# Turning q and k of batch 3 and the dilated half of batch 2 on the crossbar instead of the array

## The chip, the cores and the metric

One core of one Trainium2 chip. The metric is the device time of one launch in microseconds (us), median of several executions. PE is TensorE, DVE is VectorE, ACT is ScalarE, POOL is GpSimd, SP is SyncE. PSUM is the memory that TensorE's results go to here, SBUF the one that all other tiles of the program lie in.

## The reference

```python
# q, k, v: (8 batches, 8 heads, 576 tokens, 64)
scores = q @ k.T / 8
# heads 0-3: causal window of 32 keys; heads 4-7: 32 keys, every 4th ("dilated", window 128)
attn = softmax(where(mask, scores, -1e9))
x = (attn @ v)                   # -> (4608 tokens, 512)
h = maximum(x @ w_in, 0)         # 512 -> 2048
out = (h * h) @ w_out            # 2048 -> 512
```

All matmuls are in bf16 with f32 sums. The FFN (the last two lines) is by far the larger part; attention is woven between its pieces.

## The kernel before

Eight heads are four pairs (`e`): pairs 0 and 1 near, 2 and 3 dilated. A program in text says what is done between two FFN pieces; `|` parts the pieces. `2q1` turns and copies the queries of batch 2 (the third), pair 1; `k` does keys, `v` spreads values, `a` and `b` are the scores of the first and the second half, `o` and `p` the weighted sums of the two halves. `L3:q...` loads q and k of batch 3, and `L3:x` turns them on the crossbar (a DMA that transposes). The order within each engine's queue is the order of this program; nothing reorders it.

q and k arrive with tokens on partitions and must be turned. The kernel before does that on TensorE's array for batches 0 to 3 and by crossbar from batch 4 on (`XB = 4`):

```python
rb = [{nm: const.tile([80, ...], bf16, name=f"{nm}b{i}") for nm in "qk"} for i in range(2)]   # staging
ps_f = tile_pool(name="ps_f", bufs=4, PSUM)   # FFN sums
ps_a = tile_pool(name="ps_a", bufs=2, PSUM)   # array transposes, scores
ps_o = tile_pool(name="ps_o", bufs=1, PSUM)   # weighted sum "po"
ps_d = tile_pool(name="ps_d", bufs=1, PSUM)   # its denominators "pd"
...
def trans(b, e, nm, part):               # array: 8 transposes into one PSUM tile, then 4 copies
    ps = ps_a.tile([P, 1024], bf16, name="pa")
    copy = nc.scalar.copy if nm == "q" and e < NE // 2 else nc.vector.tensor_copy
    ...
def pv(b, e, part):                      # weighted sum and softmax denominator
    o, d = ps_o.tile(...), ps_d.tile(...)
    for ...: nc.tensor.matmul(o, v, p)           # "po"
    for ...: nc.tensor.matmul(d, ones, p)        # "pd"
    nc.scalar.activation(rec, d, Ln)
    nc.scalar.activation(rec, rec, Exp, scale=-1.0)
    nc.vector.tensor_tensor(out=xT, in0=o, in1=rec, op=mult)   # frees o
...
def step(b, code):
    if what in "qk" and b >= XB:         # crossbar: only the 4 copies, out of SBUF
        halves(e, what, (qx if what == "q" else kx)[...], 0, M, nc.vector.tensor_copy)
    elif what in "qQkK": trans(...)
```

The softmax here doesn't subtract the row's maximum and nothing guards it: scores larger than these inputs give would overflow.

Of the kernel before, what the change touches and what calls it, by code (L numbers as in the profile page):

```python
# [12 lines left out]
RES = 4  # L13
# [5 lines left out]


PROGRAM = (
    "L0:q023 L0:q00 L0:q01 0k0 L0:q10123 0q0 0q1 0k1 L0:v0pd 0a0 0q2 L0:i0 0a1 0k3 L0:v1dpr 0k2 0q3 0Q1 "
    "0K3 0a3 0Q3 0K2 0a2 0v2 0Q0 L0:i1 L0:o2 0K0 0o0 0v3 0b0 0Q2 0o2 0K1 0b3 0o1 L0:o0 0o3 0V3 0b2 0b1 | "
    "0V2 | 0p0 | 0p1 0p2 | L0:o1 0p3 L0:o3 | | | y | | | | | | | | L1:q00123 z | | | | | L1:v0dp "
    "L1:q10123 | | L2:qw0123 L1:v1dpr 1q1 1q3 | 1q2 | 1k2 | 1k1 1v3 | 1a2 | 1v2 1k0 1q0 | 1o2 | 1a0 1a1 | "
    "1k3 1o0 1o1 | 1a3 1Q0 | 1K0 1o3 | 1Q1 1K1 | 1Q2 | 1b0 | | 1Q3 1K2 L2:vwpdr | | | 2q0 | | 2k0 1V2 | "
    "1b2 1p0 | 1b1 1V3 1K3 | | 1p2 1p1 | 2a0 1b3 | 2k1 2o0 2b0 1p3 | 2q1 2k2 | | L3:qw0123 2q2 2p0 "
    "L3:vwpdr 2a1 | | | 2b1 | 2v2 2o1 2q3 2a2 | | 2p1 | 2k3 | 2b2 2o2 | 2v3 | 2a3 2p2 L4:q10123 | 2b3 | "
    "3k1 2o3 3q1 | | 3a1 L4:q00123 2p3 | 3k0 3k2 | | 3o1 | | | 3q0 3v2 | | | | 3a0 | 3b1 3k3 | | | 3p1 "
    "L4:x 3q2 | | 3b0 | 3a2 3q3 3o0 4k0 | | | 3o2 3b2 | | 3p0 3v3 | 4q1 3a3 | 3p2 4q2 4q0 | L5:q10123 3b3 "  # L30
    "| 3o3 L4:vwpdr | 4k1 | | L5:q00123 3p3 4k2 4k3 4a0 L5:vwpdr | | | 4b0 | | 4q3 | | 4o0 | | | 4a2 4v2 "
    "| 4b2 | 4a3 L5:x 4a1 | 4o2 | | | 4p2 L6:q00123 4v3 | | 4b1 | | 4p0 | | 4p1 | 5q0 5k0 | 4b3 | | | | "
    "4o1 | | 5k2 L6:q10123 4o3 | 5q2 5k1 | | 4p3 | 5q1 |"
)


# [24 lines left out]
def kernel(  # L61
# [9 lines left out]
    nc = tc.nc  # L71
    P = nc.NUM_PARTITIONS
    B, H, S, D = q.shape
# [3 lines left out]
    bf16 = mybir.dt.bfloat16  # L77
# [5 lines left out]
    NE = H // 2  # L83
# [3 lines left out]
    M = S // RES  # L87
    MS = (0, 64)
    MN = (64, M - 64)
    NT = 512  # L90
    NTILES = NTOK // NT
    XB = 4
    WHOLE = tuple(range(2, XB))
    PARTED = (0, 1)
    ADDED = 4
    RING = 4 * S
    KT = DM // P
# [2 lines left out]
    const = ctx.enter_context(tc.tile_pool(name="const", bufs=1))  # L100
# [26 lines left out]
    ]  # L127
    w_out_sb = const.tile([P, NF, DM], bf16, name="w_out_sb")
    xT = const.tile([P, KT, RING], bf16, name="xT")
    rb = [{nm: const.tile([80, 2 * H * RES * D], bf16, name=f"{nm}b{i}") for nm in "qk"} for i in range(2)]  # L130
    qT = const.tile([P, NE, RES, M], bf16, name="qT")

    qx = const.tile([P, H, 2, M], bf16, name="qx")
    kx = const.tile([P, H, 2, M], bf16, name="kx")
    kbd = const.tile([P, NE, NB, P], bf16, name="kbd")
    vbd = [const.tile([P, NE, NB, P], bf16, name=f"vbd{i}") for i in range(2)]

# [5 lines left out]
    def staged(b: int, nm: str):  # L143


        t = rb[b % 2][nm]
        if b in WHOLE:
            return t[:, :].rearrange("p (h a x) -> p h a x", h=H, a=2)
        return t[:, :].rearrange("p (a h x) -> p a h x", h=H, a=2)

    def load_qk(b: int, part, es):
        hs = slice(2 * es[0], 2 * es[-1] + 2)
        for nm, src in (("q", q), ("k", k)):
            t = staged(b, nm)
            if b in WHOLE:
                nc.gpsimd.dma_start(
                    t[0 : M // 2, hs, :, :].rearrange("p h a x -> p (h a) x"),
                    src[b, hs, :, :].rearrange("h (a p r) d -> p (h a) (r d)", a=2, r=RES),
                )
            else:  # L160
                t0, n = RES * MS[part], MN[part]
                nc.gpsimd.dma_start(  # L162
                    t[0:n, part, hs, :], src[b, hs, t0 : t0 + RES * n, :].rearrange("h (p r) d -> p h (r d)", r=RES)
                )

    def load_v(b: int, parts, which="pdr"):

# [45 lines left out]

    def cross(b: int, nm: str, part: int):

        n, m0 = MN[part], MS[part]
        nc.sync.dma_start_transpose(
            (qx if nm == "q" else kx)[:, :, :, m0 : m0 + n].rearrange("p h c m -> p (h c) m"),
            staged(b, nm)[0:n, part, :, :].rearrange("p h x -> p (h x)"),
        )  # L220

    def trans(b: int, e: int, nm: str, part: int):

        ps = ps_a.tile([P, 1024], bf16, name="pa")
        t = staged(b, nm)
        copy = nc.scalar.copy if nm == "q" and e < NE // 2 else nc.vector.tensor_copy
        if b == 0:

            m0, n = MS[part], MN[part]
            pv_ = ps[:, 0 : RES * n].rearrange("p (r m) -> p r m", r=RES)  # L230
            for r in range(RES):
                for hl in range(2):
                    nc.tensor.transpose(  # L233
                        pv_[64 * hl : 64 * hl + 64, r, :],
                        t[0:n, part, 2 * e + hl, D * r : D * r + D],
                        ident[0:n, 0:n],
                    )
            if nm == "q":
                copy(qT[:, e, :, m0 : m0 + n], pv_)
                return  # L240
            for hl in range(2):
                rows = slice(64 * hl, 64 * hl + 64)
                if e < NE // 2:
                    copy(  # L244
                        kbd[rows, e, m0 // 16 : (m0 + n) // 16, rows].rearrange("p i (m r) -> p i m r", r=RES),
                        pv_[rows, :, :].rearrange("p r (i m) -> p i m r", m=16),
                    )
                else:
                    copy(kbd[rows, e, RES * part : RES * part + RES, rows], pv_[rows, :, 0:64])  # L249
                    if part:  # L250
                        copy(
                            kbd[rows, e, 8, rows].rearrange("p (m r) -> p m r", r=RES),
                            pv_[rows, :, 64:n].rearrange("p r m -> p m r"),
                        )
            return
        if b in WHOLE:
            m0, n, pitch, cuts = 0, M, M, [(t[0:72, :, a, :], 72 * a, 72) for a in range(2)]
        else:

            m0, n, pitch, cuts = MS[part], MN[part], 80, [(t[0:80, part, :, :], 0, 80)]  # L260
        pv_ = ps[:, 0 : 4 * pitch].rearrange("p (h c m) -> p h c m", h=2, c=2)
        for hl in range(2):
            for c in range(2):
                for src, c0, w in cuts:
                    nc.tensor.transpose(  # L265
                        pv_[:, hl, c, c0 : c0 + w], src[:, 2 * e + hl, P * c : P * c + P], ident[0:w, 0:w]
                    )
        halves(e, nm, pv_[:, :, :, 0:n], m0, n, copy)
# [31 lines left out]
    def blocks(b: int, e: int, part: int):  # L300
# [3 lines left out]
        if e < NE // 2:  # L304
# [4 lines left out]
            return [(3, None, 64, 72)] + [(i, None, 16 * i, min(16 * i + 24, M)) for i in range(4, NB)]  # L309
        if b not in PARTED:  # L310
            rs = (2 * part, 2 * part + 1)
# [60 lines left out]
    def pv(b: int, e: int, part: int, spare=None, name=""):  # L372
# [8 lines left out]
        c = half_at(b, e)[0] * part  # L381
        byr = dil and b not in PARTED
        mms, dms = [], []
# [78 lines left out]
    def step(b: int, code: str):  # L462



        what, e = code[0], int(code[1])
        part = int(what in "QKVbp")
        if what in "qk" and b >= XB:
            t = qx if what == "q" else kx
            halves(e, what, t[:, 2 * e : 2 * e + 2, :, :], 0, M, nc.vector.tensor_copy)  # L470
        elif what in "qQkK":
            trans(b, e, what.lower(), part)
        elif what in "vV":
            spread_v(b, e, [part] if b in PARTED else [0, 1])
        elif what in "ab":
            scores(b, e, part, *((ps_f, "pf") if b == 0 and not part else ()))
        elif b == 0 and part and e % 2:
            pv(b, e, part, ps_a, "pa")
        elif b in PARTED and e % 2:
            pv(b, e, part, ps_f, "pf")  # L480
        else:
            pv(b, e, part)
# [140 lines left out]
    def run(code):  # L623
        if code == "y":
            for nm in "qk":
                nc.vector.memset(staged(1, nm)[64:80, 0, :, :], 0.0)
        elif code == "z":
            zero_halves(vbd[1])
        elif code[0] != "L":
            step(int(code[0]), code[1:])  # L630
        else:
            b, what, part, which = int(code[1]), code[3], code[4:5], code[5:]
            if what == "q":
                load_qk(b, None if part == "w" else int(part), [int(e) for e in which])
            elif what == "x":
                cross_all(b)
            elif what == "v":
                load_v(b, [0, 1] if part == "w" else [int(part)], which)
            else:
                (load_w_in if what == "i" else load_w_out)(int(part))  # L640
# [66 lines left out]
```

## Time and profile before

| | before |
|---|---|
| time, median of 3 runs | 319.62 us (319.12 to 319.97) |
| span of the profiled execution | 317.3 us |
| array transposes of batches 2 and 3 | 128 |

The page's slices of VectorE and ScalarE:

```profile
DVE  6785758898987987996599658965896324204400
ACT  5366735877958966686468646864686466316511
```

One slice is 7.9 us. From the 8th to the 12th slice (55 to 95 us) VectorE stands at 8 or 9 tenths and ScalarE at 5 to 9, while TensorE, shown in the prediction, stands at 9. The transposes that the change removes stand between 78.6 and 115.7 us, half of them in this stretch.

### The profile page before, as it was taken

To read this page: it belongs to the slowest core of one execution; us is meant where nothing else is said; L and a number is where in the kernel's file an instruction comes from. 1 tells how busy PE (TensorE), PEld (TensorE's weight loads), DVE (VectorE), ACT (ScalarE), POOL (GpSimd) and SP (SyncE) were. 2 spreads that over 40 slices of the span, in tenths; PEclk is the share of its full clock that TensorE was granted. 3 is DMA by queue.
4 is the path that set the end of the run, shared out by engine and by line. 5 is a ranking of instruction groups with operands and counts; after the bars stand their busy time and mean duration, and the time that the engine had idled before them with its cause. 6 is when DMAs were issued, how large, how long until landed. Compare 5 with 4: busy or idle time off the path is not lost.

```text
span 317.3 us, 6743 instructions
## 1 busy us (share of the span) xinstructions
PE 299.7 (94%) x2523; PEld 190.3 (60%) x2556; DVE 208.6 (66%) x664; ACT 195.4 (62%) x422; POOL 84.1 (27%) x130
## 2 busy tenths in 40 slices
PE   1698999999999999999999999999999999999995
PEld 1587945877965555555579755555555555445543
DVE  6785758898987987996599658965896324204400
ACT  5366735877958966686468646864686466316511
POOL 8762282367320037741271041000000000000000
PEclk9999999999999999999999999999999999999999
DMA  7999999999996619999699864352200210021022
GB/s 96 179 123 212 207 144 204 130 91 162 108 119 130 120 16 204 159 186 167 91 132 174 134 99 90 49 103 68 66 2 2 68 66 0 24 78 33 0 68 66
DMA packets 73056, 33.08 MB, mean 104 GB/s; under 512 B 44096, under 2 KB 67008, under 8 KB 73024
## 3 DMA queue, kind: packets, MB, share of 16 engines
q0 software_dynamic: 48096, 18.36, 50.3%
q1 hardware_dynamic: 24784, 14.16, 19.0%
q8 instruction: 20, 0.33, 0.4%
q10 hardware_dynamic: 144, 0.13, 0.1%
q14 instruction: 12, 0.10, 0.1%
HBM read 36.83 MB, written 9.44 MB: 146 GB/s over the span
## 4 chain that ended last, share of the span: by engine, by line
PE 88%; DVE 5%; ACT 3%; issue 2%; DMA 1%; POOL 1%; ACTq 0%; DVEq 0%; POOLq 0%
PE pf L529 38%; PE pf L561 37%; PE po L443 3%; PE pd L445 3%; PE pa L265 2%; PE pa L334 2%; PE pa L340 1%; DMA kb<-in_k_dram 1%; DVE xT L458 1%; PE pa L233 1%; DVE kbd L244 1%; DVE kbd L249 1%; ACT rec L447 1%; ACT qT L278 1%; ACT rec L448 1%
## 5 line engine op out<-in xcount | busy, mean ns | idle before, releaser
L529 PE MATMUL pf<-xT,w_in 128*128 128x256 bf16 (+1 forms) x758 | 132.9, 325 | 1.2 <-DVE xT L458 0.3
L561 PE MATMUL pf<-w_out_sb,h2T 128*128 128x512 bf16 (+1 forms) x569 | 131.0, 373 | 1.7 <-ACT osb L567 0.5
L529 PEld LDWEIGHTS <-w_in 128*128 128x128 bf16 x768 | 82.1, 114 | 35.7 <-issue 1.3
L540 ACT ACTIVATE h2T<-pf 128x512 bf16<-128x512 f32 x144 | 83.4, 597 | 24.7 <-PE pf L529 23.8
L561 PEld LDWEIGHTS <-h2T 128*128 128x128 bf16 x592 | 54.2, 98 | 53.5 <-issue 0.7
L541 DVE TENSOR_TENSOR h2T<-h2T 128x512 bf16<-128x512 bf16 x144 | 57.3, 422 | 36.0 <-ACT h2T L540 34.8
L567 ACT COPY osb<-pf 128x512 f32<-128x512 f32 (+1 forms) x37 | 21.2, 573 | 44.5 <-PE pf L561 41.5
L458 DVE TENSOR_TENSOR xT<-po,rec 128x288 bf16<-128x288 f32 (+2 forms) x56 | 25.5, 456 | 34.8 <-ACT rec L448 34.2
L447 ACT ACTIVATE rec<-pd 128x288 f32<-128x288 f32 (+2 forms) x56 | 23.1, 412 | 28.1 <-PE pd L445 28.0
L179 POOL DMA_DIRECT2D vbd<-in_v_dram x40 | 28.2, 728 | 43.8 <-PE pd L445 34.6
L344 ACT ACTIVATE pt<-pa 128x352 bf16<-128x352 f32 (+6 forms) x60 | 29.7, 502 | 8.4 <-PE pa L340 4.4
L448 ACT ACTIVATE rec<-rec 128x256 f32<-128x256 f32 (+2 forms) x64 | 28.4, 444 | 2.0
L443 PEld LDWEIGHTS <-vbd 128*128 128x128 bf16 x332 | 19.6, 99 | 10.2 <-issue 1.4
L443 PE MATMUL po<-pt,vbd 128*128 128x32 bf16 (+3 forms) x286 | 19.6, 199 | 0.7 <-DVE xT L458 0.7
L445 PE MATMUL pd<-pt,mk 128*128 128x96 bf16 (+5 forms) x172 | 18.0, 207 | 0.0
L162 POOL DMA_DIRECT2D qb<-in_q_dram x14 | 10.1, 721 | 27.0 <-PE po L443 24.6
L192 POOL DMA_DIRECT2D vd<-in_v_dram x24 | 14.7, 648 | 9.6 <-DMA kb<-in_k_dram 9.6
L278 DVE COPY qT<-qx 64x288 bf16<-64x288 bf16 x64 | 16.1, 251 | 0.8
L282 DVE COPY kbd<-kx 64x288 bf16<-64x288 bf16 x32 | 15.0, 469 | 0.4
L198 POOL DMA_DIRECT2D vbd<-in_v_dram x16 | 9.7, 617 | 17.4 <-PE pd L445 5.1
L334 PE MATMUL pa<-qT,kbd 128*128 128x96 bf16 (+2 forms) x160 | 13.8, 206 | 0.5 <-DVE kbd L244 0.4
L445 PEld LDWEIGHTS <-mk 128*128 128x128 bf16 x232 | 13.7, 99 | 0.7 <-issue 0.5
(60 smaller groups left out, 231.0 us busy)
## 6 DMA issues: line engine op xcount, KB each, us to landing
out_dram<-osb SPq DMA_DIRECT2D x18, 128.0 KB, 4.8
vd<-in_v_dram POOLq DMA_DIRECT2D x32, 64.0 KB, 5.2
w_in<-in_moe_w_in_dram POOLq DMA_DIRECT2D x2, 1024.0 KB, 9.0
w_out_sb<-in_moe_w_out_dram POOLq DMA_DIRECT2D x4, 512.0 KB, 13.5
qb<-in_q_dram POOLq DMA_DIRECT2D x6, 320.0 KB, 5.1
kb<-in_k_dram POOLq DMA_DIRECT2D x6, 320.0 KB, 6.6
vbd<-in_v_dram POOLq DMA_DIRECT2D x24, 72.0 KB, 5.8
out_dram<-osb SPq DMA_DIRECT2D x10, 160.0 KB, 2.2
```

The lines of the kernel that those rows point to most:

```text
L179: nc.gpsimd.dma_start(dst[rows, e, i0:i1, rows], v[b, 2 * e + hl, 64 * i0 : 64 * i1, :].rearrange("(i p) d -> p i d", p=64),)
L344: nc.scalar.activation(pt[:, off : off + n], ps[:, 0:n], ACT.Exp, scale=SCALE)
L443: nc.tensor.matmul(oo, vb[:, e, i, :], rh, start=(x == 0), stop=(x == len(mms) - 1), skip_group_check=True)
L445: nc.tensor.matmul(dd, ones[:, :], rh, start=(x == 0), stop=(x == len(dms) - 1), skip_group_check=True)
L447: nc.scalar.activation(rec[:, 0:n], d[:, 0:n], ACT.Ln)
L448: nc.scalar.activation(rec[:, 0:n], rec[:, 0:n], ACT.Exp, scale=-1.0)
L458: nc.vector.tensor_tensor(out=tok, in0=o if o is o3 else o[:, 0:n], in1=rec if o is o3 else rec[:, 0:n], op=ALU.mult)
L529: nc.tensor.matmul(acc[u][:, nt * x + y0 : nt * x + y1], w_in_sb[piece][:, kt, c0 : c0 + 509 : 4], xT[:, kt, t0 : t0 + y1 - y0], start=(kt ...
L540: nc.scalar.activation(hv, acc[u][:, :].rearrange("p (x n) -> p x n", x=per), ACT.Relu)
L541: nc.vector.tensor_tensor(out=hv, in0=hv, in1=hv, op=ALU.mult)
L561: nc.tensor.matmul(cur[m][:, c0:c1], h2[:, f, P * m : P * m + P], w_out_sb[:, f, c0:c1], start=(f == 0), stop=(f == NF - 1),)
L567: nc.scalar.copy(osb[:, c0:c1], cur[m][:, c0:c1])
```

## The change

Its intent: batch 3 wholly and the dilated half of batch 2 are turned by crossbar, so 96 array transposes leave TensorE. A third pair of staging buffers lets their loads come early enough; batch 2's remaining array transposes take 80 rows like batch 1's, so that there is only one layout of staging.

```diff
-    XB = 4
-    WHOLE = tuple(range(2, XB))
+    XB = 2
+    STAGE = (0, 1, 0, 2, 2, 2, 0, 1)
-    rb = [... for i in range(2)]
+    rb = [... for i in range(3)]
-    qx = const.tile(...); kx = const.tile(...)
+    qx = [const.tile(..., name=f"qx{i}") for i in range(2)]; kx = [...]      # by b % 2
 def cross(b, nm, part):
+    h0 = H // 2 if b == XB else 0                       # batch 2: dilated heads only
 def trans(...):
-        if b in WHOLE: cuts = [(t[0:72, :, a, :], 72 * a, 72) for a in range(2)]
+        if b == 2:     cuts = [(t[0:80, a, :, :], MS[a], 80) for a in range(2)]
 def step(...):
-        if what in "qk" and b >= XB:
+        if what in "qk" and (b > XB or b == XB and e >= NE // 2):
+            by_act = what == "q" and e < NE // 2 and b < ADDED         # near q of batch 3: ScalarE
 ...
+                nc.vector.memset(staged(2, nm)[64:80, 0, 0 : H // 2, :], 0.0)
 PROGRAM (loads and crossbars only; the order of attention steps is unchanged):
-  L2:qw0123 ... L2:vwpdr | | | 2q0 ... 2q1 2k2 | | L3:qw0123 2q2 2p0 L3:vwpdr ... 3q2 ... 3o3 L4:vwpdr
+  L2:q00123 L2:q10123 ... L2:vwpdr L3:q00123 L3:q10123 | L2:x | | 2q0 ... 2q1 2k2 L3:x | | 2q2 2p0 L3:vwpdr ... 3q2 L4:vwpdr ... 3o3
```

## The prediction

> **What bounds the kernel now.** I read the page first (busy shares and the slices), then the chain that ended last, then the groups by shape, then the waits, and last the order of time of the queues that start transfers.
>
> ```profile
> PE 299.7 (94%) x2523; PEld 190.3 (60%) x2556; DVE 208.6 (66%) x664; ACT 195.4 (62%) x422; POOL 84.1 (27%) x130
> PE   1698999999999999999999999999999999999995
> PEclk9999999999999999999999999999999999999999
> DMA  7999999999996619999699864352200210021022
> ...
> PE 88%; DVE 5%; ACT 3%; issue 2%; DMA 1%; POOL 1%; ACTq 0%; DVEq 0%; POOLq 0%
> ```
>
> PE is at nine tenths or more in every slice from about 32 us to the last one, at the full clock, and the chain is PE for 88%. A busy PE can hide waits, because the end of a matmul is modelled, so I checked it in the chain in order of time. In each line there: start, length, instructions.
>
> ```profile
> 50.76 0.29 PE pa L265 x8
> ...
> 99.82 0.52 PE pa L265 x16
> ...
> 211.54 2.59 PE pf L561 x12
> ```
>
> Twelve FFN matmuls of 512 columns take 2.59 us, 216 ns each, back to back. The array transposes (L265) are no different: 16 of the 72-row ones take 0.52 us, 32.5 ns each, and 8 of the 80-row ones (second batch) 0.29 us, 36 ns each. So behind the start-up (PE's one wait for a load is 6.4 us at the very start, below) nothing but PE work counts. What leaves PE's stream shortens the kernel by its back-to-back time; what leaves another engine gives nothing by itself.
>
> ```profile
> PE pa L233 <- DMA kb<-in_k_dram: 6.4, 1, 6.4
> ...
> L265 PE MATMUL pa<-mk,qb 72*128 72x72 bf16 x64 | 3.4, 196 | 0.0
> L265 PE MATMUL pa<-mk,kb 72*128 72x72 bf16 x64 | 3.2, 197 | 0.0
> ```
>
> The rows by shape say 196 ns for one such transpose. That is its latency. The last column, idle time of PE before it, is 0.0.
>
> **What the Trainium skill says.** "TensorE: Matmul & The Clock Gate", section "Back-to-back issue gap", gives N / 2.4 + 2.5 ns for a warm stream: 32.5 ns at 72 columns, 35.8 at 80, 215.8 at 512. The trace agrees (32.5, 36, 216). The same page, "Part 4: PE-mode transpose", gives 275 to 390 ns for one 128x128 transpose and says that the full clock does not engage for it; the trace does not show that cost in a stream: 197 ns of latency, 32.5 ns of pitch. "DMA: Bandwidth & Descriptors", section "Issuing engines are not separate DMA queues", says that transfers issued from any engine run on the same 16 DMA engines and interleave. So crossbar transposes compete with the loads. The trace agrees: with little beside it a crossbar occupies SP's queue 1.3 to 2.0 us, in the midst of loads up to 6.2 us.
>
> ```profile
> 100.13 1.34 SPq L217 DMA_TRANSPOSE kx<-kb  x1
> 101.65 1.76 SPq L217 DMA_TRANSPOSE qx<-qb  x1
> 103.52 1.99 SPq L217 DMA_TRANSPOSE kx<-kb  x1
> 105.61 1.97 SPq L217 DMA_TRANSPOSE qx<-qb  x1
> ...
> 138.66 6.21 SPq L217 DMA_TRANSPOSE kx<-kb  x1
> ```
>
> "VectorE: DVE Perf Modes", section "Why PSUM operands drop a tier", says that a PSUM source leaves VectorE one read port, so the copy loses its fastest mode. The rows agree in part: the contiguous copies gain some 50 ns from an SBUF source, the strided one for near keys hardly.
>
> ```profile
> L278 DVE COPY qT<-qx 64x288 bf16<-64x288 bf16 x64 | 16.1, 251 | 0.8
> L278 DVE COPY qT<-pa 64x288 bf16<-64x288 bf16 x16 | 4.9, 304 | 0.2
> L289 DVE COPY kbd<-kx 64x256 bf16<-64x256 bf16 x32 | 7.4, 230 | 0.3
> L289 DVE COPY kbd<-pa 64x256 bf16<-64x256 bf16 x16 | 4.6, 287 | 0.4
> L282 DVE COPY kbd<-kx 64x288 bf16<-64x288 bf16 x32 | 15.0, 469 | 0.4
> L282 DVE COPY kbd<-pa 64x288 bf16<-64x288 bf16 x16 | 7.7, 480 | 0.8 <-PE pa L265 0.3
> ```
>
> **The change, part by part.** I count batches from 0, so the third is batch 2.
>
> 1. Removed from PE. In the kernel before, batches 2 and 3 are turned on the array: per pair of heads and per q or k, 2 heads x 2 column halves x 2 row halves = 8 transposes, so 64 a batch (the 128 of the two 72-row rows). Batch 3 loses all 64, batch 2 its dilated half, 32. The program confirms it: 192 rows fewer on PE, 96 transposes and 96 weight loads. 96 x 32.5 ns = 3.12 us, all on the path. The order of the rest of PE's stream is the same.
> 2. Made longer on PE. The 32 transposes left for batch 2 go from 72 to 80 rows: 32 x 3.3 ns = 0.11 us back. Net of 1 and 2: 3.0 us.
> 3. VectorE. The dilated copies of batches 2 and 3 read SBUF: 16 of q save 304 - 251 = 53 ns (0.85 us), 16 of k save 57 ns (0.91 us), 8 near k copies save 11 ns (0.09 us). 16 small remainder copies may lose some 17 ns each (203 against 186, 0.27 us). Two memsets are added, half the size of the two that take 912 ns, so an estimate of 0.46 us each. Net about 0.7 us less on VectorE, which has idle time: nothing on the path.
> 4. ScalarE. Eight near q copies of batch 3 read SBUF instead of PSUM. ScalarE's PSUM copies of that shape take 391 ns, and its copies of masks from SBUF of 288 elements 431 ns, so some 0.3 us more on an engine that is 62% busy: nothing.
> 5. PSUM. Twelve turns of the two-buffer pool "pa" go away, and scores follow each other there more freely. PE's listed waits on it are a few tenths each (one of 0.2 us for ScalarE's q copy of batch 3). I give this 0.1 us.
> 6. DMA. Eight crossbar transposes are added, four of half size. The four of batch 4 begin to issue at 100.13 and end at 107.58 with few loads beside them, 7.5 us. So 7.5 us for batch 3 and, as an estimate, half of it, 3.7 us, for batch 2: 11 us of DMA work in a stretch where the DMA row shows 9s up to 95 us. No bytes of loads are added; whole-batch loads are only cut in two.
> 7. Moved. Batch 3 gets a third staging pair, so its k load no longer waits for batch 1's last transposes (2.83 us at 71 us). Batches 4 and 5 use the same pair, each after the crossbar of the one before. Batch 4's v load no longer stands behind a load of batch 5 that waited 24.6 us.
>
> Sum: 319.62 - 3.12 + 0.11 - 0.1 = 316.5 us, 1% faster. Only the removal from PE counts.
>
> **The rivals.**
>
> (a) Late crossbars: the wait for the array turns into a wait for DMA. Deadlines: VectorE begins batch 3's first k copy at 95.05; some 1 us earlier after the change, since batch 2's 32 transposes are gone.
>
> ```profile
> 67.47 1.03 POOL L156 DMA_DIRECT2D qb<-in_q_dram  x1
> 71.33 1.02 POOL L156 DMA_DIRECT2D kb<-in_k_dram  x1 [2.83 <-PE pa L265]
> ...
> 95.05 2.01 DVE L282 COPY kbd<-pa 64x288 bf16<-64x288 bf16 x4 [0.29 <-PE pa L265]
> ```
>
> Batch 3's loads can all be issued from 67.5 to about 70.5. Before, the k load issued at 71.33 held up a later transfer until 84.19, so I put the landing at 78 to 83. SP is free for them after its stores at 77. Four crossbars then need 7.5 us undisturbed and about 15 us in traffic like that at 134 to 149 (four of them, 133.78 to 148.72). So they end between 86 and 93, and in the bad case 97. The deadline is 94: most likely met, by 1 to 8 us. If missed by 1 to 3 us, VectorE and ScalarE stand still in order, scores of batch 3 come late, and PE loses most of it: 317.5 to 319.5. I give this 20%. Batch 2's crossbars have it easier: SP is idle from 59.6 to 71.3, the load has landed by about 59, and the first copy is near 79.
>
> (b) Output stores stuck behind crossbars. SP is one queue in order; the waits list already has ScalarE's output copy waiting 0.8 us for a crossbar. With three output buffers, and only two output tiles between 77 and 98, there is room. This would cost some tenths: 10%.
>
> (c) Gain beyond the removed work, because VectorE was the real limit from 60 to 90 us (the slices say 9s) and a shorter PE stream is joined by faster copies. Against it: PE is back to back there too. At most 0.5 us more: 316.0.
>
> (d) The transposes were free, hidden beside weight loads or waits, so nothing changes: 319.6. Against it: they stand in the chain with their full pitch, and nothing ran in PE meanwhile. 5%.
>
> **Range and chances.** The middle is 316.5; (c) sets the lower edge at 315.7, a small miss by (a) or (b) the upper edge at 318.0. Faster by over 2% would need 313.2, 6.4 us, twice what leaves PE: 1%. Slower by over 2% would need 326.0, a wait of nearly 10 us for a crossbar or a chain of stores: 2%. Within 2%: 97%.
>
> **What would show each step.** Right: PE has 96 transposes fewer and its busy time falls by about 3 us; the span falls by as much; the chain keeps PE near 88%, with L265 down from 2.0% to about 1.1%; after 30 us PE waits for no transfer. The dilated copies by VectorE show 230 to 250 ns. Step 6 is right if eight more crossbars appear, four at about 60 to 70 us and four at about 78 to 93, while PE keeps its 9s. (a) would show as VectorE or ScalarE idle before copies out of kx or qx with a DMA named as the releaser, between 90 and 100 us, and a PE slice under 9 there. (b) would show as ScalarE's output copy waiting for a store or crossbar by over 1 us. (d) would show as PE's idle time growing by what its work fell. My prediction is wrong if the time falls by less than 1.6 us or by more than 4.

## More of the kernel before

Groups are counted from the first `|` on, from 0.

The single buffer of `ps_o` will matter: the next weighted sum cannot begin before ScalarE's two activations and VectorE's multiplication of the one ahead are done.

## The result, and the profile after

| | before | after |
|---|---|---|
| time, first set, median of 4 | 319.76 us | 317.85 us (317.54 to 317.85) |
| ratio | | 0.9948 (0.9935 to 0.9961) |
| time, later set on another chip | 319.80 us (11 runs) | 317.88 us (6 runs), ratio 0.9951 |
| span of the profile | 317.3 us | 315.8 us |

A ratio is the mean time of one kernel's fast runs over that of the other's of the same rounds, so it is not quite the ratio of the medians. The change gains 0.5%, 1.6 to 1.9 us, where 3.1 were predicted. The page of the changed kernel:

```profile
PE 296.9 (94%) x2428; PEld 187.0 (59%) x2460; DVE 207.6 (66%) x666; ACT 195.1 (62%) x422; POOL 85.7 (27%) x134
```

TensorE's busy time fell by 2.8 us (299.7 to 296.9), about as predicted. The span fell by 1.5, so about half of the removed work came back as idle time. To see where, set the same stretch of the two kernels side by side. Lines of the order of time give start, length, engine, line of the program, operation, operands, count, and in brackets the idle time before and what ended it. In the changed kernel L257 is the array transposes (L265 before), L435 and L437 the weighted sum and its denominators (L443 and L445), L524 and L556 the two FFN matmuls (L529 and L561). TensorE, before:

```profile
84.76 0.32 PE L443 MATMUL po<-pt,vbd 128*128 128x96 bf16 x4
84.92 0.32 PE L445 MATMUL pd<-pt,mk 128*128 128x96 bf16 x4
85.07 0.43 PE L265 MATMUL pa<-mk,qb 72*128 72x72 bf16 x8
...
86.61 0.81 PE L561 MATMUL pf<-w_out_sb,h2T 128*128 128x512 bf16 x3
87.47 0.38 PE L443 MATMUL po<-pt,vbd 128*128 128x32 bf16 x6
```

and after:

```profile
84.61 0.32 PE L435 MATMUL po<-pt,vbd 128*128 128x96 bf16 x4
84.76 0.32 PE L437 MATMUL pd<-pt,mk 128*128 128x96 bf16 x4
84.92 0.32 PE L332 MATMUL pa<-qT,kbd 128*128 128x96 bf16 x4
...
85.98 1.03 PE L556 MATMUL pf<-w_out_sb,h2T 128*128 128x512 bf16 x3
87.36 0.39 PE L435 MATMUL po<-pt,vbd 128*128 128x32 bf16 x6 [0.35 <-DVE xT L450]
```

The eight transposes (0.26 us) are gone, yet from one weighted sum to the next it is 2.75 us after and 2.71 us before. In place of the transposes stands a wait. What fills the 2.75 us are the other two engines, ScalarE first, then VectorE (changed kernel):

```profile
85.22 0.65 ACT L535 ACTIVATE h2T<-pf 128x512 bf16<-128x512 f32 x1
85.70 0.45 ACT L439 ACTIVATE rec<-pd 128x256 f32<-128x256 f32 x1
86.18 0.42 ACT L440 ACTIVATE rec<-rec 128x256 f32<-128x256 f32 x1
```

```profile
85.90 0.43 DVE L536 TENSOR_TENSOR h2T<-h2T 128x512 bf16<-128x512 bf16 x1
86.25 0.60 DVE L200 COPY vbd<-vd 64x512 bf16<-64x512 bf16 x2
86.88 0.42 DVE L450 TENSOR_TENSOR xT<-po,rec 128x256 bf16<-128x256 f32 x1
```

The denominators end at about 85.1. Ln (L439) stands behind an FFN activation in ScalarE's queue and starts at 85.70, its Exp ends at 86.60, and the multiplication that frees "po" stands behind two copies of v in VectorE's queue and ends at 87.30. TensorE goes on at 87.36. That is a round trip through two queues, and TensorE's own work no longer fills it. In this kernel ScalarE is busy without a pause from 80.70 us, the first of TensorE's FFN sums that it waits for, to the end of this Exp; the part on relieving both engines comes back to that.

The second place is at 97 us. TensorE, then ScalarE, in the changed kernel:

```profile
97.33 0.32 PE L326 MATMUL pa<-qT,kbd 128*128 128x96 bf16 x4 [0.45 <-ACT qT L270]
...
99.58 1.02 PE L524 MATMUL pf<-xT,w_in 128*128 128x512 bf16 x3 [0.27 <-DVE xT L450]
```

```profile
94.75 0.41 ACT L439 ACTIVATE rec<-pd 128x288 f32<-128x288 f32 x1 [0.75 <-DVE kbd L274]
95.19 0.44 ACT L440 ACTIVATE rec<-rec 128x288 f32<-128x288 f32 x1
95.54 1.74 ACT L270 COPY qT<-qx 64x288 bf16<-64x288 bf16 x4
```

(The page puts the wait at 94.75 down to a VectorE copy; the denominators that Ln reads end at 94.71, so it is TensorE.) The q copies for the next scores stand behind an Ln and an Exp that need TensorE's last denominators, though batch 3's last crossbar left SP's queue at 87.35 and its data landed at 88.9 us (4.5 us after its start, by the view of line L209):

```profile
77.81 2.22 SPq L209 DMA_TRANSPOSE kx<-kb  x1
...
84.40 2.95 SPq L209 DMA_TRANSPOSE qx<-qb  x1
```

Batch 2's crossbars occupy SP's queue from 59.76 to 65.22, batch 3's from 77.81 to 87.35; the first copies of batch 3 begin at 94.29. Their data landed by 72.4 and 88.9 us, so no transfer is late.

**A ledger of TensorE's waits.** The bracket understates a wait, since the modelled end of the matmul ahead covers part of it. I take the distance of two starts less the pitch of the first (columns / 2.4 + 2.5 ns, the rule that the prediction compares with this trace), and count waits above 0.06 us that have a releaser, between 76 us and the end of attention:

| wait before (us) | | wait after (us) | |
|---|---|---|---|
| | | 79.3, FFN for xT | 0.24 |
| 87.1, sum for "po" | 0.21 | 86.6, sum for "po" | 0.51 |
| 97.4, scores for q copies | 0.21 | 96.5, scores for q copies | 0.61 |
| | | 98.9, FFN for xT | 0.43 |
| 125.3, sum for "po" | 0.10 | 123.7, sum for "po" | 0.19 |
| sum | 0.51 | sum | 1.98 |

3.12 us of transposes, less 0.11 for the 80-row shape, less 1.47 of new waits is 1.54. To compare this without the start-up, whose length varies by up to 1.5 us between executions, I use the *rest*: from the start of one weighted sum near 76 us (the same sum in all kernels, at 75.95 to 77.41 us) to the end of the span. The rest is 317.27 - 75.95 = 241.3 us before and 315.77 - 76.09 = 239.7 after, 1.6 less; a second profile of the changed kernel on another chip gave 239.8. So the ledger closes to about 0.1 us. A rest below is read from one profile of each kernel; these two are all that is known of its noise.

### The profile page after: what moved, and what is told of

Its sections match the earlier page's. It is cut to its first block, busy times and chain, and to the rows that moved or that the text cites. A ratio compares the mean times of both kernels' runs of the same rounds, so it can differ in the third digit from the quotient of the medians.

```text
span 315.8 us, 6569 instructions
## 1 busy us (share of the span) xinstructions
PE 296.9 (94%) x2428; PEld 187.0 (59%) x2460; DVE 207.6 (66%) x666; ACT 195.1 (62%) x422; POOL 85.7 (27%) x134
## 4 chain that ended last, share of the span: by engine, by line
PE 85%; ACT 6%; DVE 4%; issue 2%; DMA 1%; POOL 1%; ACTq 0%; DVEq 0%; POOLq 0%
PE pf L556 37%; PE pf L524 37%; PE po L435 3%; PE pd L437 3%; PE pa L326 2%; PE pa L332 1%; DMA kb<-in_k_dram 1%; ACT h2T L535 1%; ACT qT L270 1%; DVE xT L450 1%; PE pa L257 1%; ACT rec L439 1%; PE pa L225 1%; ACT rec L440 1%; DVE kbd L236 1%
## 5 line engine op out<-in xcount | busy, mean ns | idle before, releaser
L524 PE MATMUL pf<-xT,w_in 128*128 128x256 bf16 (+1 forms) x758 | 133.0, 325 | 1.7 <-DVE xT L450 0.8
L556 PE MATMUL pf<-w_out_sb,h2T 128*128 128x512 bf16 (+1 forms) x570 | 131.1, 373 | 1.7 <-ACT osb L562 0.5
L524 PEld LDWEIGHTS <-w_in 128*128 128x128 bf16 x768 | 82.2, 113 | 36.9 <-issue 2.2
L556 PEld LDWEIGHTS <-h2T 128*128 128x128 bf16 x592 | 54.2, 98 | 53.7 <-issue 0.7
L171 POOL DMA_DIRECT2D vbd<-in_v_dram x40 | 28.3, 727 | 62.8 <-PE pd L437 33.5
L439 ACT ACTIVATE rec<-pd 128x288 f32<-128x288 f32 (+2 forms) x56 | 23.1, 412 | 27.7 <-PE pd L437 26.9
L435 PEld LDWEIGHTS <-vbd 128*128 128x128 bf16 x332 | 19.7, 99 | 10.8 <-issue 1.7
L270 DVE COPY qT<-qx 64x288 bf16<-64x288 bf16 x80 | 20.1, 251 | 1.1
L435 PE MATMUL po<-pt,vbd 128*128 128x32 bf16 (+3 forms) x286 | 19.6, 199 | 1.1 <-DVE xT L450 1.0
L154 POOL DMA_DIRECT2D qb<-in_q_dram x18 | 13.3, 739 | 21.9 <-issue 10.7
L274 DVE COPY kbd<-kx 64x288 bf16<-64x288 bf16 x40 | 18.8, 470 | 0.6
L437 PE MATMUL pd<-pt,mk 128*128 128x96 bf16 (+5 forms) x172 | 18.0, 207 | 0.0
L437 PEld LDWEIGHTS <-mk 128*128 128x128 bf16 x232 | 13.7, 99 | 0.7 <-issue 0.5
L337 DVE TENSOR_TENSOR pt<-pt,mask_p 128x352 bf16<-128x352 bf16 (+3 forms) x32 | 11.9, 372 | 3.0 <-ACT pt L336 2.8
```

Of the source, the lines that this page charges most:

```text
L171: nc.gpsimd.dma_start(dst[rows, e, i0:i1, rows], v[b, 2 * e + hl, 64 * i0 : 64 * i1, :].rearrange("(i p) d -> p i d", p=64),)
L270: copy(qT[rows, e, :, m0 : m0 + n].rearrange("p (c j) m -> p j c m", j=2)[:, jj, :, :], src)
L435: nc.tensor.matmul(oo, vb[:, e, i, :], rh, start=(x == 0), stop=(x == len(mms) - 1), skip_group_check=True)
L437: nc.tensor.matmul(dd, ones[:, :], rh, start=(x == 0), stop=(x == len(dms) - 1), skip_group_check=True)
L439: nc.scalar.activation(rec[:, 0:n], d[:, 0:n], ACT.Ln)
L524: nc.tensor.matmul(acc[u][:, nt * x + y0 : nt * x + y1], w_in_sb[piece][:, kt, c0 : c0 + 509 : 4], xT[:, kt, t0 : t0 + y1 - y0], start=(kt ...
```

## The experiments

Eighteen runs, with profiles and medians, compared with runs of the kernel before on the same chip. All results passed the tolerance, also those that are wrong on purpose.

| run | time | ratio (95%) | rest |
|---|---|---|---|
| changed kernel again | 317.88 | 0.9951 (0.9935 to 0.9968) | 239.8 |
| dummy | 319.33 | 0.9989 (0.9972 to 1.0006) | 241.4 |
| b3_only | 318.42 | 0.9960 (0.9943 to 0.9977) | 240.4 |
| b2_only | 329.14 | 1.0292 (1.0271 to 1.0312) | |
| b2_only_late_load | 319.85 | 1.0001 (0.9983 to 1.0018) | 241.3 |
| late_x | 328.75 | 1.0288 (1.0261 to 1.0316) | |
| q1_first | 317.40 | 0.9926 (0.9908 to 0.9943) | 239.4 |
| tuned_a | 317.88 | 0.9951 (0.9929 to 0.9974) | 239.9 |
| tuned_b | 319.50 | 0.9987 (0.9963 to 1.0011) | 240.9 |
| dve_plus | 318.99 | 0.9981 (0.9961 to 1.0001) | 240.3 |
| before_dve_plus | 320.47 | 1.0021 (0.9999 to 1.0042) | 241.9 |
| dve_minus | 318.48 | 0.9967 (0.9944 to 0.9990) | 239.8 |
| pool_q | 318.08 | 0.9951 (0.9928 to 0.9975) | 239.2 |
| act_minus | 318.09 | 0.9951 (0.9936 to 0.9965) | 239.7 |
| all_minus | 316.86 | 0.9924 (0.9905 to 0.9942) | 238.8 |
| before_all_minus | 319.19 | 0.9989 (0.9972 to 1.0006) | 241.0 |
| spare_p1 | 317.52 | 0.9939 (0.9922 to 0.9955) | 238.9 |
| v2_later | 317.56 | 0.9940 (0.9922 to 0.9958) | 239.3 |

### Dummy: the transposes' time put back, without their function

```diff
         if what in "qk" and (b > XB or b == XB and e >= NE // 2):
+            if b < ADDED:
+                ps = ps_a.tile([P, 1024], bf16, name="pa")
+                for x in range(8):
+                    nc.tensor.transpose(ps[:, 72*x : 72*x + 72], mk[0:72, 0:P], ident[0:72, 0:72])
```

> The changed kernel with 96 array transposes of a constant put back on PE where the removed ones stood (8 ahead of each crossbar-fed copy, into a PSUM turn that nothing reads); crossbars, copies, loads stay as in the changed kernel. Theory P (the missing gain is PE arriving early and waiting for ScalarE and VectorE chains that the transposes used to fill): the waits near 79, 87, 96 and 99 us fill up again, so adding 3.1 us of PE work costs only 1.6 to 1.9 us: 319.4 to 319.9, the time of the kernel before. Theory S (the crossbars themselves, by DMA traffic, slower copies or the memsets, cost 1.4 us wherever PE stands): the full 3.1 us come on top, 320.7 to 321.2.

The rest is 241.4 us, that of the kernel before to 0.1. 3.1 us of array work that nobody needs cost 1.7 (by the times 1.2 to 1.5, a little under the expected 1.6). So the half gain is not the price of the crossbars or of the new copies: in the kernel before, too, half of the transposes stood where TensorE would else have waited. In the dummy's trace the sum after the same eight transposes shows no wait:

```profile
85.94 0.42 PE L466 MATMUL pa<-mk 72*128 72x72 bf16 x8
...
88.13 0.39 PE L435 MATMUL po<-pt,vbd 128*128 128x32 bf16 x6
```

### Each batch's part alone

b3_only: crossbar for batch 3 alone; batch 2's dilated heads stay on the array (80 rows).

```diff
-        if what in "qk" and (b > XB or b == XB and e >= NE // 2):
+        if what in "qk" and b > XB:
 PROGRAM: - L2:x          (memsets widened to all of batch 2's heads, not shown)
```

> Crossbar for batch 3 alone; batch 2 goes wholly over the array with the 80-row shape. Removes 64 x 32.5 = 2.08 us of PE work and adds 64 x 3.3 ns = 0.21 us. Theory P: the waits near 96 and 99 us (0.84 us together more than before) stay, those near 79 and 87 us do not appear: about 318.6 (318.3 to 318.9). Without any new waits it would be 317.8.

b2_only: crossbar for batch 2's dilated heads alone.

```diff
-    STAGE = (0, 1, 0, 2, 2, 2, 0, 1)
+    STAGE = (0, 1, 0, 1, 2, 2, 0, 1)
-        if what in "qk" and (b > XB or b == XB and e >= NE // 2):
+        if what in "qk" and (b > 3 or b == XB and e >= NE // 2):
 PROGRAM: - L3:x          (batch 3 takes batch 2's 80-row branch in trans, not shown)
```

> Crossbar for the dilated half of batch 2 alone; batch 3 over the array with the 80-row shape, from the second staging pair. Removes 32 x 32.5 = 1.04 us of PE work, adds 96 x 3.3 = 0.32 us. Theory P: the waits near 79 and 87 us take back 0.54: 319.5 (319.2 to 319.9), nearly nothing gained. Without any new waits it would be 319.0.

This run is a mistake of mine, and shows why the change brings a third staging pair: I left batch 3's loads where they are, so they overwrite a pair that batch 1's last transposes still read, and these wait for the load (and take the wrong batch's keys). TensorE's waits list it (total, times, longest):

```profile
PE pa L257 <- DMA kb<-in_k_dram: 6.6, 1, 6.6
```

b2_only_late_load: the same, with batch 3's loads moved behind batch 1's transposes (`L3:q00123 L3:q10123` from group 36 to group 50).

> The kernel with the crossbar for the dilated half of batch 2 alone, mended: batch 3's loads, which share a staging pair with batch 1, now come after batch 1's last array transposes (in the run before they came ahead of them, so that these waited 6.8 us for the loads and turned batch 3's keys in place of batch 1's). Removes 1.04 us of PE work, adds 0.32. Theory P, with the waits near 79 and 87 us taking back 0.54: 319.2 to 319.9. Without new waits 319.0.

Batch 3's part alone gains 0.9 us of rest where 64 transposes take 2.08 (0.91 came back as waits, 0.21 by the 80-row shape of batch 2); batch 2's part alone gains nothing where 32 take 1.04. In the latter's trace the ledger's waits sum to 1.11 us (0.24, 0.50, 0.18 and, at 125 us, 0.19), 0.6 more than before, and all its 96 remaining transposes of the two batches have the 80-row shape, 0.3 us: what was removed in batch 2 came back.

### Crossbars that really are late

```diff
 PROGRAM: - L3:x in group 48
          + L3:x in group 61
```

> The changed kernel with the four crossbars of batch 3 issued later by 13 groups, behind two output stores, so from about 92.8 instead of 77.8 us. By the prediction's deadline (first copies at 94) this is too late: the last of the four lands at about 101, ScalarE and VectorE stand before copies out of qx and kx with a DMA as releaser, and PE loses 4 to 6 us: 321.5 to 324. If the crossbars had much more slack than I think, no change: 317.8.

It cost 11 us against the changed kernel, about twice the expected. It shows what the prediction's rival (a) looks like, and that the changed kernel has nothing of it:

```profile
107.57 0.45 PE L326 MATMUL pa<-qT,kbd 128*128 128x96 bf16 x4 [10.00 <-ACT qT L270]
```

ScalarE itself waited 9.4 us for the crossbar there. That it cost twice the expected has its reason in this trace: the expectation took the end of a crossbar in SP's queue for the arrival of its data. The last of the four left the queue at 101.03, as expected, but its data landed 6.7 us after its start, at 105.7, and ScalarE's copies began at 105.77:

```profile
L209 SPq DMA_TRANSPOSE qx<-qb x1: 2051/2051/2051, 99.0 to 99.0; - x1
...
DMA to landing us min/median/max: 6.7/6.7/6.7
```

### The order in ScalarE's queue

q1_first moves one word, so that the copies of q stand ahead of the Ln and Exp that need TensorE:

```diff
 PROGRAM, group 62:
-  3k1 2o3 3q1
+  3q1 3k1 2o3
```

> The changed kernel with one word moved: ScalarE's q copy of batch 3, pair 1, stands first in its group, ahead of the softmax denominators of the last head pair of batch 2, for which ScalarE waits 0.75 us. Theory P (order in a queue): the PE waits of 0.6 us at 96.5 and 0.43 us at 98.9 shrink by 0.4 to 0.9 us in all: 317.0 to 317.4. Rival T (ScalarE and VectorE are at their throughput there, so order does not matter) or late crossbars: 317.7 to 318.0, or more if the crossbar data were not there yet.

As expected: 317.40 us, and the wait of 0.61 us is down to 0.22, now for "po"; the rest is 0.3 us shorter. ScalarE and TensorE in this run:

```profile
93.86 1.74 ACT L270 COPY qT<-qx 64x288 bf16<-64x288 bf16 x4
95.63 0.41 ACT L439 ACTIVATE rec<-pd 128x288 f32<-128x288 f32 x1
```

```profile
96.68 0.32 PE L326 MATMUL pa<-qT,kbd 128*128 128x96 bf16 x4
```

The copies now run 1.68 us earlier and the scores start 0.65 us earlier. That one is an order in a queue.

tuned_a moves three more words (near k of pair 1 of batch 2 behind 1p3; the spread 2v2 behind 2o1; 3k2 from group 65 to 62):

> The changed kernel with four words moved, all of them copies that PE no longer feeds or that stand ahead of what PE waits for: q copy of batch 3 pair 1 first in its group; k copy of batch 3 pair 2 three groups earlier, into VectorE's 1.5 us of idle time; k of batch 2 pair 1 after the head pairs of batch 1 and 2 that PE waits for at 79 us; v spread of batch 2 after the head pair that PE waits for at 87 us. Theory P (order in the queues): all four waits (0.24, 0.5, 0.6, 0.43 us) mostly go, the time nears the 316.5 that the removed PE work alone would give: 316.2 to 316.9. Theory T (throughput of VectorE and ScalarE): no better than the one-word kernel, 317.2 to 317.6.

A miss. The rest is 239.9. The wait at 79 us is gone and that at 87 us down to 0.09, but others stand at 84.7 (0.43), 89.9 (0.32) and 99.1 us (0.55). tuned_b, the same with the q copies 3q1 on VectorE in group 60:

> As the kernel with four words moved, but q of batch 3 pair 1 is copied by VectorE, where four copies out of the crossbar's buffer take about 1 us against 1.7 us on ScalarE, and two groups earlier. Theory P: 316.0 to 316.9, about the same or 0.2 us better; if VectorE is the limit there, worse than the other by 0.3 us or more.

Worse, by 1.0 us of rest: TensorE's scores now wait 0.98 us for VectorE's k copies. From these two I drew theory V, that VectorE's throughput is the pace between 76 and 93 us.

### More and less work on VectorE

dve_plus and before_dve_plus put four VectorE copies that nobody reads into the changed kernel and into the kernel before (written shorter here):

```diff
+        if (b, code) == (2, "q2"):
+            for x in range(4):
+                nc.vector.tensor_copy(scr[0:64, :], mk[0:64, 0:288])     # 64x288 bf16
```

> The changed kernel with four harmless VectorE copies (64x288 bf16, a constant into a scratch tile that nobody reads) put ahead of the q copies of pair 2 of the third batch, at about 82 us. Nothing waits for their result. If the real q copies of that shape (251 ns each) are a guide they add 0.6 to 1.0 us of VectorE work and no TensorE work at all. Theory V (between 76 and 93 us VectorE has no slack, so its own time is the pace there): the kernel gets 0.5 to 1.0 us slower than the changed kernel, ratio to before 0.9965 to 0.9985. Theory P (TensorE's stream is the bound and VectorE work is hidden, as the prediction had it): ratio stays at 0.9945 to 0.9955.

> The same four VectorE copies in the kernel before, at the same place in its program. If VectorE already had no slack there before the change (it was busy 15.93 us of 17 between 76 and 93 us), this too costs 0.3 to 1.0 us: ratio 1.001 to 1.003. If VectorE only became the bound through the change, the ratio is 1.000 within 0.0007.

They take 0.9 us in each (228 and 226 ns each), and cost 0.6 us of rest in both kernels (239.7 to 240.3 and 241.3 to 241.9; the times' intervals are too wide to show so little). Before the change, too, VectorE's work there was not free, against the prediction's steps 3 and 4. The copies lie in the first of two round trips from one "po" to the next, and both trips grow, from 3.89 to 4.14 and from 2.75 to 2.97 us (before: 3.90 to 4.29 and 2.71 to 2.97). dve_minus, the other direction, leaves out eight copies:

```diff
-            halves(e, what, t[...], ...)
+            if (b, code) not in ((2, "q2"), (2, "q3")):
+                halves(e, what, t[...], ...)
```

> The changed kernel without the q copies of pairs 2 and 3 of the third batch on VectorE (eight copies of 251 ns, 2.0 us); the scores of these heads are then made from the previous batch's queries, so the result is wrong on purpose (it may still pass the tolerance). TensorE's work is the same. Theory V: the waits of TensorE at about 79 and 87 us (0.24 and 0.5 us) go or shrink, and the time falls by 0.3 to 0.8 us against the changed kernel: ratio 0.9920 to 0.9938. Theory P: ratio stays at 0.9945 to 0.9955. More than 0.9 us would mean that VectorE holds TensorE also where the trace shows no wait.

Theory V falls. With 2.0 us less on VectorE the rest is 239.8 and every wait stands as before, the one at 87 us with 0.50 us. VectorE simply idles:

```profile
83.01 0.49 DVE L450 TENSOR_TENSOR xT<-po,rec 128x320 bf16<-128x320 f32 x1 [0.41 <-ACT rec L440]
```

This multiplication now waits for ScalarE's reciprocal, so taking VectorE's copies away ahead of it brings nothing; the other four copies stand behind the multiplication of the wait at 87 us and never delayed it. Being busy and being the pace are two things. pool_q moves these eight copies to GpSimd, on top of q1_first:

> The version with the q copies of pair 1 of the fourth batch put first in its group (317.40), and with the q copies of pairs 2 and 3 of the third batch moved from VectorE to GpSimd, which has no other work there but issuing loads. If only VectorE's throughput counts, it gains another 0.3 to 0.8 us on 317.40: 316.6 to 317.1, ratio 0.990 to 0.992. If GpSimd's copies are so slow that the scores wait for them, or slow VectorE's copies down beside them, it is no better than 317.4 and may be worse by 1 us or more.

No gain beyond q1_first: 0.2 us of rest, which is one wait of 0.28 us at 113 us that q1_first's profile shows and this one does not. On GpSimd such a copy had a median of 428 ns. It agrees with dve_minus.

### Both engines relieved, in both kernels

all_minus and before_all_minus leave out the copies of 2k1, 2q1, 2q2, 2q3 and 3q1 (a guard around `halves`); act_minus leaves out those of 2q1 alone.

```diff
+        if now[0] not in ('2k1', '2q1', '2q2', '2q3', '3q1'):
             _halves(e, nm, t, m0, n, copy)
```

> The changed kernel without five of its copy steps between 76 and 97 us: near k of pair 1 and dilated q of pairs 2 and 3 of the third batch (VectorE, 2.0, 1.0 and 1.0 us), near q of pair 1 of the third and of the fourth batch (ScalarE, 1.6 and 1.7 us). TensorE has the same work. Wrong on purpose: the scores of these heads are made from an older batch's q or k. Theory L (TensorE's new waits are round trips through the in-order queues of ScalarE and VectorE): the waits at 79, 87, 97 and 99 us, 1.8 us in sum, go, and the time is 316.0 to 316.6, about 3.0 us under the same cut in the kernel before. Rival O (something else, a transfer or a PSUM turn, holds TensorE): at most 0.6 us under the changed kernel.

> The same five copy steps left out of the kernel before, whose array transposes all stay. Its trace has only two waits of 0.2 us there, so theory L expects 319.2 to 319.6 (ratio 0.9980 to 0.9995), and a difference to the changed kernel with the same cut of 2.8 to 3.2 us, which is what the 96 transposes take. Rival O expects a difference of 1.6 to 2.1 us, as without the cut.

> The changed kernel without only the near q copies of pair 1 of the third batch on ScalarE (1.6 us at 79 us; scores wrong on purpose). If ScalarE's queue alone makes the wait at 87 us (0.5 us), it goes and the ratio is 0.993 to 0.9935; if it takes both engines, or VectorE's order behind it, the ratio stays at 0.9945 to 0.9955. The wait at 79 us, which comes ahead of it, should stay at 0.24 us.

> The changed kernel again, as a baseline on this chip: ratio 0.9935 to 0.9961 as measured at first.

act_minus gains nothing, but it is no test of ScalarE's load at 87 us: the copies that it leaves out stand ahead of a wait of ScalarE's for TensorE, and in act_minus that wait (1.97 us, 0.16 in the changed kernel) takes up their time. With all five gone, the same change is worth 2.2 us of rest (241.0 less 238.8), between what theory L (2.8 to 3.2) and rival O (1.6 to 2.1) wanted. The ledger says why. The waits at 79 and 97 us are gone, as theory L has it, but the one at 87 us stands as it was, and one of 0.32 us stands at 99:

```profile
88.43 0.39 PE L440 MATMUL po<-pt,vbd 128*128 128x32 bf16 x6 [0.34 <-DVE xT L455]
```

By the ledger's rule all_minus has 1.12 us of waits (with 0.10 and 0.20 at 119 and 124 us) and before_all_minus 0.20: 3.12 - 0.11 - 0.92 = 2.09, against 2.2 measured. What stays at 87 us is, by the traces, ScalarE's work. From the FFN sum at 81 us that it waits for to the end of the Exp that the multiplication needs, ScalarE does 13 instructions with no idle time over 0.03 us between them. They take 5.89 to 5.91 us in all 20 profiles, before and after the change, and all_minus left out none of them:

```profile
81.77 1.08 ACT L541 ACTIVATE h2T<-pf 128x512 bf16<-128x512 f32 x2 [1.73 <-PE pf L530]
...
83.94 2.05 ACT L541 ACTIVATE h2T<-pf 128x512 bf16<-128x512 f32 x4
...
87.26 0.42 ACT L445 ACTIVATE rec<-rec 128x256 f32<-128x256 f32 x1
```

VectorE's multiplication begins 0.28 us later, behind the copies of v. From that FFN sum to the next "po" TensorE itself had 6.7 us of work before the change and has 6.2 after it, 16 transposes less. In dummy and b3_only, where it has 6.7 us or more, ScalarE's stretch is as long, TensorE does not wait, and one "po" follows the other after 2.50 and 2.53 us in place of 2.75. No run takes work out of this stretch of ScalarE, so that ScalarE's load is the pace there is read from the traces and not shown by an experiment.

### The buffer of the weighted sum

spare_p1 gives that one sum and its denominators two buffers of the FFN's ring, on top of q1_first:

```diff
-        elif b in PARTED and e % 2:
+        elif b in PARTED and e % 2 or (b, code) == (2, "p1"):
             pv(b, e, part, ps_f, "pf")
```

> The version with the q copies of pair 1 of the fourth batch first in their group (317.40), in which one weighted sum (third batch, pair 1, second half) writes two buffers of the FFN's PSUM ring in place of the single buffer of its own. Theory B (the turn of the single buffer, 2.7 us from one sum to the next, makes the wait at 87 us): that wait goes, and the time is 316.8 to 317.1, unless the FFN's accumulators, two fewer for that while, wait in turn: then a wait on an FFN tile stands at 85 to 89 us in its place and the time stays at 317.2 to 317.8. If the wait at 87 us stays though the buffer is another, theory B falls.

The wait at 87 us is gone; the sum follows the one ahead after 2.25 us, back to back:

```profile
85.08 0.32 PE L435 MATMUL po<-pt,vbd 128*128 128x96 bf16 x4
...
87.33 0.39 PE L435 MATMUL pf<-pt,vbd 128*128 128x32 bf16 x6
```

So the turn of the one "po" buffer made this wait. Of the 0.50 us, 0.25 came back at 91.9 us, at the turn after next. The rest, 238.9, is the shortest of the kernels that compute the right thing, 0.5 us under q1_first's. The time itself doesn't show it: 317.52 against 317.40, on other chips, with intervals of some 0.5 us to either side.

v2_later, also on top of q1_first, leaves the buffer and takes one VectorE step (the copies of v) out of the turn:

```diff
 PROGRAM: - group 54: 2v2 2o1 2q3 2a2      + group 54: 2o1 2q3 2a2
          - group 56: 2p1                  + group 56: 2p1 2v2
```

> The same version (317.40), with one VectorE step (the spread of v of pair 2 of the third batch, 0.60 us) moved from just ahead of the multiplication that releases the weighted sum's buffer to just behind the next sum. Theory B: the multiplication then starts when ScalarE's reciprocal is there, 0.25 us earlier, the turn shortens from 2.75 to about 2.5 us and the wait at 87 us falls from 0.5 to about 0.25 us; time 317.0 to 317.3. If later sums wait for the moved step in its place, the time stays at 317.4.

The turn falls to 2.49 us and the wait at 87 us to 0.25, as expected; the multiplication now begins 0.03 us behind ScalarE's Exp. A wait of 0.35 us at 89.4 us for the moved copies takes its place, which the expectation's last sentence allowed for: 317.56 us.

No version beats q1_first (317.40) beyond the noise; it is itself 0.45 us under the changed kernel, with intervals that overlap.

## Why the prediction was right or wrong

Right: the direction, and each count. Step 1: 96 transposes left, TensorE's busy time fell by 2.8 us. Step 2: batch 2's 32 remaining transposes went from 32.5 to 36 ns each, 0.1 us. Steps 3 and 4, as sizes: VectorE lost 1.0 us (predicted 0.7); ScalarE's eight copies from SBUF took 428 ns (estimate 431). Step 6: eight crossbars, 5.5 and 9.5 us of SP's queue (predicted 3.7, and 7.5 to 15), batch 3's ending at 87.35, where I had 86 to 93. Part of this is luck: step 6 and rival (a) count to the end in SP's queue, and the data landed later, at 88.9 us here; the slack of 5.4 us hid the slip, which late_x laid open. Rival (a) did not come, nor did (b): no wait of ScalarE's output copy for a transfer reaches 0.8 us. The time, 317.85, lies within the range, but near its upper edge and for another reason than the one given for that edge.

Wrong: the sentence "What leaves PE's stream shortens the kernel by its back-to-back time; what leaves another engine gives nothing by itself", and with it "nothing on the path" in step 3 and "nothing" in step 4. The term of the sum that was mis-sized is TensorE's waits behind the change. I put them at -0.1 us (step 5); they measured +1.47: at the places that the change thinned out, TensorE waits for ScalarE and VectorE, whose work there did not shrink along with its own. The dummy shows the same from the other side: 3.1 us of array work are worth 1.7.

How the reading went wrong: I checked the chain at 50, 99 and 211 us and found TensorE back to back. At 84 us, in the kernel before, the same view reads:

```profile
by line: DVE h2T L541 26.8%; PE pf L561 17.3%; DVE vbd L208 16.0%; DVE pt L345 11.2%; DVE xT L458 8.7%; issue 8.1%; PE po L443 7.7%; PE pd L445 4.5%; PE pa L265 1.3%
...
83.93 0.24 DVE pt L345
84.17 1.34 DVE h2T L541 x4
...
86.99 0.44 DVE xT L458
87.43 0.04 issue
87.47 0.38 PE po L443 x6
```

From 83.93 to 87.43 the chain is VectorE's alone, and it hands over to TensorE at the very sum that later waits. TensorE was at its nine tenths because its work filled the round trip but for 0.21 us. After the change the same view, at the same place, has ScalarE first:

```profile
by line: ACT h2T L535 31.0%; PE pf L556 21.6%; issue 16.5%; DVE vbd L200 11.4%; DVE xT L450 8.7%; PE po L435 7.7%; PE pd L437 4.5%; DVE h2T L536 0.7%
```

Of rival (c), VectorE as the real limit, I had expected a bonus; the truth was a cap, set by the work of ScalarE and VectorE together as far as the traces tell. Rival (d), "hidden beside waits", had 5% and was half true.

One reading of the skill in the prediction needs mending: section "Back-to-back issue gap" gives N / 2.4 + 2.5 ns as the gap of an isolated matmul, not of a stream. That a stream follows it too, 216 ns at 512 columns, is a finding of this trace.

The Trainium skill bears on both mechanisms. Its page "Perfetto Trace Analysis", section "Matmuls", says that independent matmul groups should rotate through PSUM banks so that their evacuation overlaps the next group; "PSUM — Partial Sum Buffer", section "Engine vs sequencer instructions", says that the queues of ScalarE, VectorE and GpSimd are strictly first in, first out. The runs agree: a second buffer removed a wait of 0.50 us (spare_p1), and another place in the queue took one of 0.61 us down to 0.22 (q1_first).

Left open: the whole of the waits was not removed in one kernel; the parts of the one at 79 us (0.24, gone in all_minus and tuned_a, where VectorE's near k copies no longer stand ahead) and at 99 us were not tried alone, nor was less work on ScalarE between 81 and 87 us.

## What to carry to other kernels

Work removed from a saturated engine is worth its time only as far as no stretch of other engines' work around it takes as long: before crediting it, follow each single-buffered result through the queues that free it, with all that stands ahead in them, and compare that time with the work left in between. Look at the chain in just the stretch that the change touches, not at its average or at a few places. A busy engine is proved to be the pace only by adding and by removing work: here adding 0.9 us cost 0.6, and removing 2.0 us gained nothing. And work taken out ahead of an engine's own wait (act_minus) only lengthens that wait; it has to come out of the stretch behind it. The end of a transfer in its queue is not its landing.

## What the Trainium skill lacked or had wrong

- "TensorE: Matmul & The Clock Gate", "Part 4: PE-mode transpose", gives 275 to 390 ns for one 128x128 transpose, says that the full clock does not engage for it, and gives no figure for a stream. Here smaller ones (72 and 80 columns), among other matmuls at a granted clock of 0.998 and above, had 196 to 199 ns of latency and streamed every 32.5 and 36 ns.
- The same page, "Back-to-back issue gap", gives about 131 ns for a matmul of 512 columns in the stream of a real kernel. Here twelve in a stream took 216 ns each.
- "Perfetto Trace Analysis", "Optimization Strategy", tells how to find gaps on the limiting engine. That a gap can be absent only because work fills it, so that removing 3.1 us of work gains 1.6, no page says.
